# A RetNet-and-MoE kernel: the first two batches' attention by 256-token spans in 64x64 tiles

## The chip, the core and the metric

The kernel runs on one core of a Trainium2 chip. The core has a matrix engine (PE, TensorE, with its weight loads shown apart as PEld), a vector engine (DVE), an activation engine (ACT), GpSimd (POOL), and SyncE (SP), which issues DMAs here. PE reads SBUF and writes PSUM; DVE and ACT bring results from PSUM to SBUF. The metric is device time in microseconds of one execution. Three runs of the kernel before gave 306.0, 306.02 and 306.26 us, median 306.02.

## What is computed

Retention (attention with a decay instead of a softmax) over 8 batches, 8 heads, 576 tokens and 64 elements per head, and then a feed-forward layer on all 4608 tokens, with 512 model and 2048 inner elements:

```python
def _attn_ref(q, k, v):
    scores = scale * np.matmul(q, k.transpose(0, 1, 3, 2))
    gamma = 1.0 - 2.0 ** (-5.0 - np.arange(H, dtype=np.float32))
    rel = pos[:, None] - pos[None, :]
    Dmat = np.where(rel >= 0, gamma[:, None, None] ** rel[None, :, :], 0.0)
    return np.matmul(scores * Dmat[None, :, :, :], v)
...
    x = attn_out.transpose(0, 2, 1, 3).reshape(B * S, H * D)
    h = x @ w_in
    g = h * (1.0 / (1.0 + np.exp(-beta * h)))
    return g @ w_out
```

All inputs and the output are float32; the matmuls run in bfloat16.

## The kernel before

**Retention by chunks.** The decay factors into a gain on q (`gq`, which falls with the token's position) and its inverse on v (`gv`), so that inside a batch only a mask is left. The first 512 tokens of a batch are four chunks of 128 tokens. For a chunk, PE transposes q and k (`t_q` L297, `t_k` L304, tile `T`), forms the scores of keys against queries per head (`a_sc` L317, tile `sc`), and DVE multiplies them by the mask on their way from PSUM (`R`, L332). The outputs (`a_O` L364, tile `O`) are v against `R`, plus a "cross" term (`a_cross` L352): q against the state, which is the sum of k times v over all earlier chunks. The state (`a_st` L390, tile `st`) is accumulated in PSUM and after each chunk copied to `sbds` (in two blocks, L416). `a_x` (L380) brings the outputs to `xT`, the input of the layer. The last 64 tokens of every batch form blocks of their own ("tails") at the end; from batch 2 on, q and k are transposed by DMA, and the work has functions of its own (`a_O4`, `a_cross4`, `x4`).

**Tiles on PE.** Scores have 64 rows to contract, so they use half of the array's rows, two at a time (64x128). Outputs have 64 columns (128x64, two at a time). Transposes, cross and the state of the first two batches use the whole array (128x128). Later batches' cross terms use 64x64, four at a time.

**The layer.** `up(m, fo)` (L466) makes one 128-row slice of the hidden layer for 512 tokens of block m: four matmuls 128x512, then one ACT instruction (`gT`, L475). There are 16 of them per block. `down(m, ms, f0, fn)` (L499) adds `fn` of the 16 products for output rows `ms`; the last one evicts `po` to `ot` and stores it. For batch 0, `up_pair` (L479) makes fo 0 and 1 together, half of the contraction at a time; the downs of batch 0 run for three row blocks abreast (`down_rows` L593) while w_out arrives, and the fourth follows. The ups of batch 1 for fo 0 to 9 run on two chunks (256 columns) at a time, so that they can start when half of its retention is done.

**Loads.** SP's one queue carries all loads and stores in program order: q of batch 0, its k and v (eight pieces of 256 KB: one chunk, all heads, a token per partition, 256-byte runs), w_in (4 MB in pieces of 256 columns), then w_out (four of 1 MB), q, k and v of batch 1 and so on. k is cast and v gets its gain on POOL (`pre`, L277 and L259), q gets its gain on DVE for the first two batches (`pre_q`, L251). w_in is cast by POOL (L185) and, with halves exchanged for odd `ko`, by DVE (L188); w_out is scaled by 1/beta on DVE, POOL and ACT (`cast_w_out`, L195).

**Order.** Each engine takes its instructions in the order of the code. Batch 0 is written out step by step (L540 to 584). After that, `fill` is a list of ups and downs that PE works through, and `streams` hold all other steps, each with a place in the fill list; `merged` (L526) issues a step ahead of the first fill whose number is not below that place. `d0` is the number of the first down of batch 0, `u1` that of the first up of batch 1, `base[n]` those of later blocks. PSUM has eight banks: `mm` 3 (ups, downs), `sc` 2, `O` 2, `st` 1.

Of the kernel before, what the change touches and what calls it, by code (L numbers as in the profile page):

```python
# [19 lines left out]
def kernel(  # L20
# [21 lines left out]
    PC = P // CB  # L42
    TL = S - MB
# [23 lines left out]
    NQ = 6  # L67
    E = CB
# [4 lines left out]
    def load_q(b, us=(0, 1)):  # L73
# [6 lines left out]
        for u in us:  # L80
            w = slice(u * HP, (u + 1) * HP)
            nc.sync.dma_start(t[:, w].rearrange("p h i d -> p h (i d)"),  # L82
                              q[b, w, :MB, :].rearrange("h (p i) d -> p h (i d)", i=CB))

# [12 lines left out]
    ahead = [(0, 0), (0, 1), (1, 0), (1, 1), (2, 0), (3, 0), (2, 1), (3, 1)]  # L97
    keys_first = [(0, 0), (1, 0), (0, 1), (1, 1), (2, 0), (3, 0), (2, 1), (3, 1)]
# [13 lines left out]
    for n, j in ahead:  # L112
        load_kv(n, (j,))
# [7 lines left out]
    pos = consts.tile([P, 2, CB + 1], F32, name="pos")  # L121
    for j, (step, mul) in enumerate(((1, CB), (P, 1))):
        nc.gpsimd.iota(pos[:, j, :CB], pattern=[[step, CB]], base=0, channel_multiplier=mul,
                       allow_small_or_imprecise_dtypes=True)
        for x in range(2):
            nc.gpsimd.iota(pos[x * TL:(x + 1) * TL, j, CB:], pattern=[[0, 1]], base=MB, channel_multiplier=1,
                           allow_small_or_imprecise_dtypes=True)
    lscale = consts.tile([P, 1], F32, name="lscale")
    nc.vector.memset(lscale[:], math.log(scale))
    lg = consts.tile([P, 2, CB + 1, H], F32, name="lg")  # L130
    for h in range(H):
        nc.vector.tensor_scalar(lg[:, :, :, h], pos[:], math.log(1.0 - 2.0 ** (-5.0 - h)), None, ALU.mult)
    gq = consts.tile([P, CB + 1, H], F32, name="gq")
    gv = consts.tile([P, CB + 1, H], F32, name="gv")
    nc.scalar.activation(gq[:], lg[:, 0], ACT.Exp, bias=lscale[:])
    nc.scalar.activation(gv[:], lg[:, 1], ACT.Exp, scale=-1.0)
# [6 lines left out]

    causal = consts.tile([P, P], BF16, name="causal")
    nc.gpsimd.memset(causal[:], 1.0)
    nc.gpsimd.affine_select(out=causal[:], in_=causal[:], pattern=[[1, CB], [CB, PC]], compare_op=ALU.is_ge,
                            fill=0.0, base=0, channel_multiplier=-1)
# [23 lines left out]
    def load_w_in(g):  # L171
# [4 lines left out]
        for w in (slice(0, 2), slice(2, KO)) if g < 2 else (slice(0, KO),):  # L176
            nc.sync.dma_start(t[:, w], w_in_r[:, w, f0:f0 + fn])  # L177
        wts[g] = t

    def cast_w_in(g):  # L180
        t = wts[g]
        f0, fn = pieces[g]
        for ko in range(KO):
# [150 lines left out]
    def split(i):  # L334
        return i in (CB - 1, CB + 1)
# [392 lines left out]
```

## Time and profile before

| | |
|---|---|
| median of three runs | 306.02 us |
| the profiled execution's own time | 305.54 us |
| its span, first to last instruction | 303.83 us |
| granted PE clock | 1.00 |
| PE busy | 293.4 us, 97% |
| ACT, DVE, POOL busy | 134.1, 108.0, 99.9 us |
| first up of the layer starts | 18.46 us |
| first down of batch 0 starts | 32.96 us |
| first up of batch 1 starts | 51.11 us |
| first down of batch 1 starts | 68.01 us |
| DMA, 0 to 60 us | 16.98 MB, mean 283 GB/s |

A line of the timeline gives the start, the busy time of the merged group, the engine, the line of the code, the operation, what it writes and reads, and how many instructions are in it; brackets give the idle time before it and what ended that. A matmul's own time (0.22 us for 128 columns, 0.38 for 512) is mostly latency: consecutive ones overlap, so the distance of their starts tells what one costs.

### The profile page before, as it was taken

Reading aid. Unit: us, or ns where it says so; the run is one execution under the profiler, and the core shown is the slowest. Engines: PE = TensorE matmul, PEld = TensorE weight load, DVE = VectorE, ACT = ScalarE, POOL = GpSimd, SP = SyncE. Lnnn points to the kernel's source line nnn. Section 1 sums busy time; section 2 is a strip of 40 time slices with the busy share of each in tenths; the row PEclk is TensorE's granted clock in tenths of the full one; section 3 lists DMA queues with packets and bytes.
Section 4 is the critical chain, followed back from the end, with each engine's and each line's share of the span. In section 5 each row is a group of like instructions: output and inputs, shape, how many; then the busy total and the mean of one; then the engine's idle time right before and its main releaser. Section 6 shows DMA issues by size and latency. Waiting matters only on the chain.

```text
span 303.8 us, 5689 instructions
## 1 busy us (share of the span) xinstructions
PE 293.4 (97%) x2311; PEld 151.3 (50%) x2345; DVE 108.0 (36%) x202; ACT 134.1 (44%) x227; POOL 99.9 (33%) x138
## 2 busy tenths in 40 slices
PE   7799999999999999999999999999999999999995
PEld 5544456854544454445444544454455544444444
DVE  6588566504640433133222413151346510020012
ACT  5567546781147313741374127511771058107700
POOL 4666317552840723350308030942342000000000
PEclk9999999999999999999999999999999999999999
DMA  8999999999999999908982889997996110131011
GB/s 210 219 344 363 385 252 244 237 189 243 173 249 265 233 190 230 262 12 158 252 219 66 156 226 243 214 187 184 185 200 112 60 45 0 32 73 35 2 69 69
DMA packets 129210, 53.86 MB, mean 177 GB/s; under 512 B 109968, under 2 KB 122656, under 8 KB 129184
## 3 DMA queue, kind: packets, MB, share of 16 engines
q1 hardware_dynamic: 129152, 53.49, 78.4%
q8 instruction: 18, 0.29, 0.4%
q14 instruction: 8, 0.07, 0.1%
q10 hardware_dynamic: 32, 0.01, 0.0%
HBM read 36.71 MB, written 9.44 MB: 152 GB/s over the span
## 4 chain that ended last, share of the span: by engine, by line
PE 87%; DMA 6%; SPq 4%; issue 1%; POOL 1%; DVE 0%; POOLq 0%
PE po L506 41%; PE ph L473 36%; SPq L94 3%; DMA wt<-in_moe_w_out_dram 3%; PE sc L327 3%; DMA wt<-in_moe_w_in_dram 2%; PE O L441 2%; PE st L402 2%; PE O L453 1%; SPq L177 1%; POOL w_out_sb L200 1%; PE O L376 0%; PE st L405 0%; SPq L82 0%; PE T L307 0%
## 5 line engine op out<-in xcount | busy, mean ns | idle before, releaser
L475 ACT ACTIVATE gT<-ph,beta_sb 128x512 bf16<-128x512 f32 (+1 forms) x152 | 99.5, 659 | 82.2 <-PE ph L473 81.7
L506 PE MATMUL po<-w_out_sb,gT 128*128 128x512 bf16 (+2 forms) x591 | 127.1, 368 | 2.1 <-issue 1.3
L473 PE MATMUL ph<-xT,w_in_sb 128*128 128x512 bf16 (+1 forms) x592 | 125.1, 365 | 0.8 <-issue 0.2
L473 PEld LDWEIGHTS <-w_in_sb 128*128 128x128 bf16 x608 | 58.4, 98 | 63.0 <-DVE w_in_sb L188 0.9
L506 PEld LDWEIGHTS <-gT 128*128 128x128 bf16 x608 | 56.8, 98 | 63.9 <-issue 0.6
L332 DVE TENSOR_TENSOR R<-sc,causal 128x512 bf16<-128x512 f32 x72 | 45.0, 684 | 81.4 <-PE sc L327 80.3
L513 DVE COPY ot<-po 128x512 f32<-128x512 f32 (+2 forms) x34 | 22.4, 657 | 77.2 <-PE po L506 74.4
L277 POOL CAST kn<-kvn 128x512 bf16<-128x512 f32 x32 | 19.5, 612 | 55.5 <-DMA kvn<-in_k_dram 55.1
L259 POOL TENSOR_TENSOR vn<-kvn,gv 128x512 bf16<-128x512 f32 x32 | 33.3, 1042 | 13.1 <-DMA kvn<-in_v_dram 6.3
L251 POOL TENSOR_TENSOR qs<-qn,gq 128x512 bf16<-128x512 f32 x24 | 24.3, 1042 | 35.1 <-DMA qn<-in_q_dram 35.1
L408 ACT CAST sbq<-st 128x256 bf16<-128x256 f32 x18 | 6.6, 369 | 35.8 <-PE st L402 35.8
L461 DVE CAST xT<-O 128x512 bf16<-128x512 f32 x20 | 12.7, 685 | 20.2 <-PE O L453 20.2
L327 PE MATMUL sc<-qT,kT 64*128 64x128 bf16 x256 | 10.8, 218 | 0.7 <-ACT kT L308 0.6
L188 DVE CAST w_in_sb<-wt 64x256 bf16<-64x256 f32 x32 | 10.7, 334 | 1.4 <-DMA wt<-in_moe_w_in_dram 0.3
L461 ACT CAST xT<-O 128x512 bf16<-128x512 f32 x8 | 4.7, 587 | 13.4 <-PE O L453 13.4
L327 PEld LDWEIGHTS <-kT 64*128 64x128 bf16 x288 | 8.2, 94 | 3.8 <-issue 1.7
L185 POOL CAST w_in_sb<-wt 128x256 bf16<-128x256 f32 x16 | 7.2, 469 | 5.3 <-DMA wt<-in_moe_w_in_dram 5.3
L402 PEld LDWEIGHTS <-kn 128*64 128x64 bf16 x192 | 5.1, 110 | 7.6 <-issue 6.4
L212 PE MATMUL ph<-warm 128*128 128x128 f32 (+1 forms) x24 | 6.5, 405 | 1.2 <-DVE warm L119 1.2
L441 PE MATMUL O<-R,vn 128*64 128x128 bf16 x224 | 7.7, 220 | 0.0
L402 PE MATMUL st<-vn,kn 128*64 128x64 bf16 x192 | 7.4, 200 | 0.0
L266 POOL TENSOR_TENSOR kn<-tln,gq 128x512 bf16<-128x512 f32 x4 | 4.2, 1042 | 9.8 <-DMA tln<-in_q_dram 5.9
(69 smaller groups left out, 103.4 us busy)
## 6 DMA issues: line engine op xcount, KB each, us to landing
qn<-in_q_dram SPq DMA_DIRECT2D x16, 512.0 KB, 5.8
kvn<-in_k_dram SPq DMA_DIRECT2D x32, 256.0 KB, 5.1
kvn<-in_v_dram SPq DMA_DIRECT2D x32, 256.0 KB, 5.0
out_dram<-ot SPq DMA_DIRECT2D x31, 256.0 KB, 2.8
wt<-in_moe_w_out_dram SPq DMA_DIRECT2D x4, 1024.0 KB, 9.7
wt<-in_moe_w_in_dram SPq DMA_DIRECT2D x6, 512.0 KB, 8.6
out_dram<-ot SPq DMA_DIRECT2D x9, 128.0 KB, 2.4
wt<-in_moe_w_in_dram SPq DMA_DIRECT2D x4, 256.0 KB, 5.8
```

The lines of the kernel that those rows point to most:

```text
L251: e.tensor_tensor(batch[b]["qs"][:, cs, hs], q_tiles[b][:, hs, cs].rearrange("p h i d -> p i h d"), gq[:, cs, hs].unsqueeze(3).to_broadcas ...
L259: nc.gpsimd.tensor_tensor(live[i]["vn"][:], kv_tiles.pop(i)[:, 1], gains(gv, c), ALU.mult)
L277: nc.gpsimd.tensor_copy(kn[:, c % 2], t[:, 0])
L327: nc.tensor.matmul(view(sc[j][:, p, :]), L["kT"][r, p, :], rhs, start=True, stop=True, skip_group_check=True)
L332: nc.vector.tensor_tensor(R[:, j], sc[j][:], m_b, ALU.mult)
L402: nc.tensor.matmul(st[j * D:(j + 1) * D, p, :D], L["kn"][:, 2 * p + j, :], L["vn"][:, 2 * p + j, :], start=(c == 0 and p == 0), stop=True, ...
L441: nc.tensor.matmul(out4(i, p, hh), L["vn"][:, 2 * p + j, :], rhs if b is None else rhs.rearrange("k (i s) -> k i s", i=CB), start=c % 2 == ...
L461: (nc.scalar.copy if n == 1 else nc.vector.tensor_copy)(to, O.rearrange("k p i s -> k p (i s)") if b is None else O[:])
L473: nc.tensor.matmul(ph, w_in_sb[:, ko, fo * P:(fo + 1) * P], xts[m][:, ko, :, w], start=(ko == 0), stop=(ko == KO - 1))
L475: nc.scalar.activation(gts[m][:, fo, :, w], ph, ACT.Silu, scale=beta_sb[:, fo:fo + 1])
L506: nc.tensor.matmul(po[:, :nn], gT[:, fo, ms, :], w_out_sb[:, fo, n0:n0 + nn], start=(fo == 0), stop=(fo == FO - 1))
L513: (nc.scalar.copy if m == 0 else nc.vector.tensor_copy)(ot, po[:, :nn])
```

## The change

For the first two batches the unit of loading and of retention becomes a span of 256 tokens, with two neighbouring tokens in each partition (`W` = 256). The low 64 partitions hold the span's first chunk, the high 64 its second.

- Loads: k and v of a span come in runs of 512 bytes; for batch 0 by four heads at a time (256 KB), for batch 1 all heads at once (512 KB). q of batch 1 is loaded by span too. For batch 1, span 0 is loaded ahead of the last quarter of w_out. w_in's first piece comes in six DMAs that exchange the halves on the way, so all its casts are on POOL; w_out comes two rows of blocks at a time.
- Scores (`sc_span`) and outputs (`O_span`) use 64x64 tiles, four at a time, 64 instructions each per batch. One `cut` mask replaces `causal` for these.
- State: batch 0 accumulates it over one half of the rows at a time (`st_first`). Batch 1 sums each prefix anew (`st_terms`, `st_span`, `st_end`) in 64x64 and 128x64 tiles.
- In batch 0, one half of the last v is only cast, on ACT, and its gain goes on that half's k instead.
- The first two ups of batch 0 run on the first span alone (`up_part`) inside the retention of the second; the other 256 columns follow as the first fill. The downs of batch 0 run by rows, four abreast (the fourth in bank `st`), with two of their evictions on ACT and two on DVE.
- All 16 ups of batch 1 run on 256 columns at a time. Several steps of batch 2's preparation move behind `u1`.

The diff, cut to its core:

```diff
+    def load_span(b, j, cc, hs):
+        if (b, j, cc) not in spans:
+            spans[b, j, cc] = stage.tile([P, H, 2, D], F32, name="kvn", tag="kvn", bufs=NQ)
+        nc.sync.dma_start(spans[b, j, cc][:, hs].rearrange("p h i d -> p h (i d)"),
+                          (k, v)[j][b, hs, cc * W:(cc + 1) * W, :].rearrange("h (p i) d -> p h (i d)", i=2))
...
-    for n, j in ahead:
-        load_kv(n, (j,))
+    for cc in range(2):
+        for j in range(2):
+            for g in range(2):
+                load_span(0, j, cc, both[g])
...
+    def cut_of(b):
+        n = CB if b == 0 else 2
+        nc.gpsimd.memset(cuts[b][:], 1.0)
+        for h in range(2):
+            r = slice(h * D, (h + 1) * D)
+            nc.gpsimd.affine_select(out=cuts[b][r], in_=cuts[b][r], pattern=[[-1, 2], [1, n], [n, P // n]],
+                                    compare_op=ALU.is_ge, fill=0.0, base=0, channel_multiplier=-2)
...
+        if g == 0:
+            for ko in range(KO):
+                for a, b, n in ((0, D, D), (D, 0, D)) if ko % 2 else ((0, 0, P),):
+                    nc.sync.dma_start(t[a:a + n, ko], moe_w_in[ko * P + b:ko * P + b + n, f0:f0 + fn])
+        else:
+            for w in (slice(0, 2), slice(2, KO)) if g < 2 else (slice(0, KO),):
+                nc.sync.dma_start(t[:, w], w_in_r[:, w, f0:f0 + fn])
...
+    def t_k(b, cc, ps, tag, e):
+        kn, kT = pair[b, cc][:2]
+        T = psum.tile([P, 2, len(ps), P], BF16, name="T", tag=tag, bufs=BANKS[tag])
+        for i in range(2):
+            for n, p in enumerate(ps):
+                nc.tensor.transpose(T[:, i, n, :], heads(kn[:, i], p), ident[:])
+        evict(e, kT[:, :, ps[0]:ps[-1] + 1, :], T[:])
...
+    def sc_span(b, cc, g, tags):
+        kT = pair[b, cc][1]
+        Rs[b, cc, g] = R = sb.tile([P, 2, 2, 2, P], BF16, name="R", tag="R", bufs=4)
+        sc = [psum.tile([P, 2, 2, P], F32, name="sc", tag=tag, bufs=BANKS[tag]) for tag in tags]
+        for n, i in ((n, i) for n in range(2) for i in range(2)):
+            p = 2 * g + n
+            for j, h in ((0, 0), (1, 1), (0, 1), (1, 0)):
+                r = slice(j * D, (j + 1) * D)
+                nc.tensor.matmul(by(b, sc[j][h * D:(h + 1) * D, n, i, :]), kT[r, i, p, h * D:(h + 1) * D], q_span(b, 2 * cc + h, r, p),
+                                 start=True, stop=True, skip_group_check=True)
+        for j in range(2):
+            nc.vector.tensor_tensor(R[:, j], sc[j][:], cuts[b][:].unsqueeze(1).to_broadcast([P, 2, 2, P]), ALU.mult)
...
+    def O_span(b, cc, g):
+        vn, R = pair[b, cc][2], Rs[b, cc, g]
+        for n, i in ((n, i) for n in range(2) for i in range(2)):
+            p = 2 * g + n
+            for j, h in ((0, 0), (1, 1), (0, 1), (1, 0)):
+                r, hh = slice(h * D, (h + 1) * D), j ^ p % 2
+                key, o = region(b, 2 * cc + h, p)
+                nc.tensor.matmul(o[hh * D:(hh + 1) * D], vn[r, i, 2 * p + j, :], by(b, R[r, j, n, i, :]),
+                                 start=begins(key, (hh,)), stop=False, skip_group_check=True)
...
+    def st_first(c, es):
+        if c == 0:
+            states[0] = psum.tile([P, HP, P], F32, name="st", tag="st", bufs=1)
+        st, (kn, _, vn), r = states[0], pair[0, c // 2], (low, high)[c % 2]
+        for i in range(2):
+            for p in range(HP):
+                nc.tensor.matmul(st[:, p, :], kn[r, i, 2 * p:2 * p + 2].rearrange("k h d -> k (h d)"),
+                                 vn[r, i, 2 * p:2 * p + 2].rearrange("k h d -> k (h d)"), start=begins(("st", 0), (0,)) if p + c + i == 0 else False,
+                                 stop=True, skip_group_check=True)
+        if c < CB - 1:
+            blocks_of(sbds[c], st, es, False)
...
+    def st_terms(x, terms):
+        st, key = states[1]
+        for p in range(HP):
+            for d, r in terms:
+                kn, _, vn = pair[1, d]
+                for i in range(2):
+                    for j in range(2):
+                        nc.tensor.matmul(st[j * D:(j + 1) * D, x, p, :], kn[r, i, 2 * p + j, :], vn[r, i, 2 * p + j, :],
+                                         start=begins(key, (j,)), stop=True, skip_group_check=True)
+    def st_span(cc, es):
+        tag = "st" if cc else "O"
+        states[1] = (psum.tile([P, 2, HP, D], F32, name="st", tag=tag, bufs=BANKS[tag]), ("st", 1, cc))
+        if cc:
+            st_terms(0, [(0, rows), (1, low)])
+            blocks_of(sbds[2], states[1][0][:, 0], es, True)
+        else:
+            st_terms(0, [(0, low)])
+            st_terms(1, [(0, rows)])
+            for x in range(2):
+                blocks_of(sbds[x], states[1][0][:, x], es, True)
+    def st_end(e):
+        st_terms(0, [(1, high)])
+        evict(e, ends[1][:], states[1][0][:, 0])
...
+    def up_part(c0, fos, kos):
+        if 0 not in gts:
+            gts[0] = sb.tile([P, FO, CB, P], BF16, name="gT", tag="gT", bufs=2)
+        w = slice(c0 * PC, (c0 + 2) * PC)
+        for fo in fos:
+            if kos[0] == 0:
+                phs[fo] = psum.tile([P, CB, 2 * PC], F32, name="ph", tag="mm", bufs=3)
+            for ko in kos:
+                nc.tensor.matmul(phs[fo][:], w_in_sb[:, ko, fo * P:(fo + 1) * P], xts[0][:, ko, :, w],
+                                 start=(ko == 0), stop=(ko == KO - 1))
+            if kos[-1] == KO - 1:
+                nc.scalar.activation(gts[0][:, fo, :, w], phs[fo][:], ACT.Silu, scale=beta_sb[:, fo:fo + 1])
...
-        (nc.scalar.copy if m == 0 else nc.vector.tensor_copy)(ot, po[:, :nn])
+        (nc.scalar.copy if m == 0 and ms % 2 == 0 else nc.vector.tensor_copy)(ot, po[:, :nn])
...
     warm_up(5)
     betas()
     betas_safe()
     for n in range(4):
         pre_q(0, n)
+    t_q(0, 0, "O", A)
     warm_up(1, 128)
+    t_q(0, 1, "mm", V)
+    pre_span(0, 0, 0, g0, Z)
+    t_k(0, 0, lo2, "mm", A)
+    pre_span(0, 0, 0, g1, Z)
+    warm_up(1, 128)
+    sc_span(0, 0, 0, ("sc", "sc"))
+    t_k(0, 0, hi2, "mm", A)
+    pre_span(0, 1, 0, g0, Z, True)
+    warm_up(1, 128)
+    sc_span(0, 0, 1, ("O", "O"))
+    pre_span(0, 1, 0, g1, Z, True)
     warm_up(2, 128)
+    new_span_O(0, 0, ("sc", "sc"))
+    O_span(0, 0, 0)
+    pre_span(0, 0, 1, g0, Z)
+    st_first(0, (A, A))
+    O_span(0, 0, 1)
+    t_k(0, 1, lo2, "mm", V)
+    pre_span(0, 0, 1, g1, Z, True)
+    x_span(0, 0, (V, None))
+    cross_span(0, 1)
+    sc_span(0, 1, 0, ("O", "O"))
+    pre_span(0, 1, 1, g0, Z, True)
+    st_first(1, (A, A))
+    t_k(0, 1, hi2, "mm", A)
+    x_span(0, 0, (None, A))
     warm_up(1, 128)
+    pre_span(0, 1, 1, g1, A)
+    sc_span(0, 1, 1, ("mm", "mm"))
     cast_w_in(0)
+    new_span_O(0, 1, ("sc", "sc"))
+    O_span(0, 1, 0)
+    st_first(2, (A, A))
+    cross_span(0, 2)
+    up_part(0, (0, 1), (0, 1))
+    O_span(0, 1, 1)
+    cross_span(0, 3)
+    x_span(0, 1, (V, A))
+    up_part(0, (0, 1), (2, 3))
     cast_w_in(1)
+    st_first(3, (A, A))
...
+    fill = [F(up_part, 2, (0, 1), range(KO))] + [F(up, 0, fo) for fo in range(2, FO)]
     d0 = len(fill)
+    def down_row(n):
+        for fo, ms in [(n, ms) for ms in range(4)] if n < FO - 2 else [(fo, 2 * (n - FO + 2) + x) for x in range(2) for fo in (FO - 2, FO - 1)]:
             down(0, ms, fo, 1)
 
+    fill += [F(down_row, n) for n in range(FO)]
 
     u1 = len(fill)
+    NH = FO
+    fill += [F(up, 1, fo, 2 * x, 2) for x in range(2) for fo in range(NH)]
+    fill += [F(up, 1, fo) for fo in range(NH, FO)]
     fill += [F(down, 1, ms, f0) for ms in range(MB // P) for f0 in range(0, FO, 4)]
+    base = {1: u1 + NH}
...
+    def span_rest(cc):
+        if cc:
+            cross_span(1, 2)
+        cross_span(1, 2 * cc + 1)
+        x_span(1, cc, (V, V if cc else A))
...
+               [(d0 + 7, F(pre_q, 1, 0)), (d0 + 7, F(pre_q, 1, 1)), (d0 + 8.5, F(t_q, 1, 0, "O", V)),
+                (d0 + 8.6, F(pre_span, 1, 0, 0, both[0], A)), (d0 + 8.6, F(pre_span, 1, 0, 0, both[1], A)),
+                (d0 + 9.5, F(t_k, 1, 0, (0, 1), "O", V)), (d0 + 10.5, F(t_k, 1, 0, (2, 3), "O", A)), (d0 + 10.51, F(span_sc, 0, 0)),
+                (d0 + 10.6, F(pre_span, 1, 1, 0, both[0], Z, True)), (d0 + 10.6, F(pre_span, 1, 1, 0, both[1], Z, True)),
+                (d0 + 11, F(span_sc, 0, 1)), (d0 + 12, F(cast_w_out, WG - 1)), (d0 + 13.5, F(span_out, 0, 0)),
+                (d0 + 13.9, F(span_out, 0, 1)), (d0 + 13.95, F(st_span, 0, (A, V))), (d0 + 15.5, F(span_rest, 0))],
+               [(u1, F(pre_q, 1, 2)), (u1, F(pre_q, 1, 3)), (u1 + 2, F(t_q, 1, 1, "O", V)),
+                (u1 + 1, F(pre_span, 1, 0, 1, both[0], Z)), (u1 + 2.1, F(pre_span, 1, 0, 1, both[1], V)),
+                (u1 + 3, F(t_k, 1, 1, (0, 1), "O", V)), (u1 + 4, F(t_k, 1, 1, (2, 3), "O", V)), (u1 + 5, F(span_sc, 1, 0)),
+                (u1 + 5.1, F(pre_span, 1, 1, 1, both[0], Z, True)), (u1 + 5.1, F(pre_span, 1, 1, 1, both[1], Z, True)),
+                (u1 + 6, F(span_sc, 1, 1)), (u1 + 10, F(span_out, 1, 0)), (u1 + 12, F(st_span, 1, (V, V))),
+                (u1 + 13, F(span_out, 1, 1)), (u1 + 14, F(span_rest, 1)), (u1 + NH + 2, F(st_end, A))]]
```

## What was predicted ahead of the run

> **What bounds the kernel.** I read the page's head first, then the timeline of PE, then the starts of single matmuls.
>
> ```profile
> span 303.8 us, 5689 instructions
> PE 293.4 (97%) x2311; PEld 151.3 (50%) x2345; DVE 108.0 (36%) x202; ACT 134.1 (44%) x227; POOL 99.9 (33%) x138
> ...
> PEclk9999999999999999999999999999999999999999
> ```
>
> PE is busy nearly all the time at full granted clock, so the time is the head before the first up, the PE work after it, and whatever PE waits. The timeline of PE gives the joints:
>
> ```profile
> 17.89 0.40 PE L405 MATMUL st<-vn,kn 128*128 128x128 bf16 x4
> 18.46 0.59 PE L488 MATMUL ph<-xT,w_in_sb 128*128 128x512 bf16 x2 [0.17 <-ACT xT L386]
> 19.22 1.41 PE L488 MATMUL ph<-xT,w_in_sb 128*128 128x512 bf16 x5 [0.17 <-issue]
> 20.47 12.66 PE L473 MATMUL ph<-xT,w_in_sb 128*128 128x512 bf16 x55
> 32.96 1.55 PE L506 MATMUL po<-w_out_sb,gT 128*128 128x512 bf16 x6
> 34.66 9.22 PE L506 MATMUL po<-w_out_sb,gT 128*128 128x512 bf16 x41 [0.15 <-POOL w_out_sb L200]
> ```
>
> The head lasts 18.5 us; from 20.47 the ups of fo 2 to 15 run. Consecutive 128x512 matmuls start 0.2157 us apart, so these 56 would end at 32.55 instead of 32.96 (0.41 of waits on w_in), and the six at 32.96 would end at 34.25 instead of 34.66 (0.41 on w_out). What ends the waits of the head, from the timelines of POOL, DVE and ACT:
>
> ```profile
> 13.47 0.61 POOL L277 CAST kn<-kvn 128x512 bf16<-128x512 f32 x1 [0.57 <-DMA kvn<-in_k_dram]
> 14.70 2.19 POOL L259 TENSOR_TENSOR vn<-kvn,gv 128x512 bf16<-128x512 f32 x2 [0.61 <-DMA kvn<-in_v_dram]
> 14.46 2.69 DVE L332 TENSOR_TENSOR R<-sc,causal 128x512 bf16<-128x512 f32 x4 [1.13 <-PE sc L327]
> 13.39 0.58 ACT L308 COPY kT<-T 128x512 bf16<-128x512 bf16 x1 [1.22 <-PE T L307]
> 13.87 0.76 ACT L416 CAST sbd<-st 64x256 bf16<-64x256 f32 x2
> ```
>
> POOL waits for loads: pieces of 256 KB come 1.2 us apart (7.47, 8.67 ... 13.47, 14.70). ACT and DVE wait for PE. The head follows the loads.
>
> **The loads.** Runs of 256 bytes move at about 217 GB/s (the 40 slices over the first 60 us), w_in's of 1 KB at about 348, w_out's of 2 KB at 385. No load here has 512-byte runs. Bounds: 1.2 us per piece (nothing gained) and 0.68 (256 KB at 385 GB/s). Per engine a 256-byte run takes 18.9 ns and a 1 KB run 47.1; the line between gives 28.3 for 512 bytes, 0.9 us per piece, which I take. The last v lands about 13.4 instead of 15.8, and w_in follows 2.4 us earlier.
>
> **The head, walked.** I took the new order engine by engine: each starts when its last instruction and its inputs are done, about 0.05 us after them. Durations by row: R 0.645 (two in 1.29), kT 0.58 on ACT and 0.42 on DVE, state to sbd two in 0.76, xT 0.58 on ACT and 0.69 on DVE, POOL 0.61 plain and 1.04 with a gain. The same walk over the order before gives the first up at 18.3 (trace 18.46) and L473 at 20.3 (20.47), so I trust it to some tenths. After:
>
> The first half's keys are turned by 9.05, its R is done at 10.9, the second half's at 12.2 (DVE runs through). The outputs of the second half wait for that, and only behind them on PE stand the second span's transposes (12.6, though their keys were cast at 11.5). On DVE then come kT (to 13.4), xT (14.1) and R (15.4). On ACT come the first state (12.3 to 13.0), the second (14.45 to 15.2), and behind it kT's other half, xT and the last v, 0.58 each, to 16.95: that v landed at 13.4. It releases the third state (17.0), then the first-span ups (17.8), the last outputs and cross (18.6), xT (to 19.6), the other half of fo 0 and 1 (19.9) and L473's work at 20.8, against 20.3. ACT starts back-to-back work up to 0.09 us before the last one's end (14.79 and 15.28 in its timeline, 0.58 each), which gives back 0.2. So the head is **+0.3**, whether a piece takes 0.68 or 1.1 us: the load time falls, but the chain over PE, ACT and DVE takes its place. At 1.2 us it is +0.7. The early w_in ends the 0.41 of waits, w_out in halves the other 0.41.
>
> At nothing I cost the finer DMAs (an issue takes 0.5 us, SP is done with k and v by 6 us), w_in's first casts on POOL (done about 15.3, wanted at 17.8), two more Exp of 0.2 to 0.3 (under the wait for q, which ends at 4.74), the masks moved among the ups (POOL idles there) and batch 2's moved preparation (loaded by 58, wanted at 72). If such a cover goes, the cost is its own duration. Span 0 of batch 1 is loaded ahead of w_out's last quarter, so that one lands about 41.5; row 12 wants it at 45.
>
> **Batch 1 on PE.** Start-to-start, from busy times less one instruction's own (24 in 0.53, one 0.22): T, cross and old st 56 ns, sc in 64x128 26.5, O in 128x64 28, 64x64 tiles 13.6, 64-column st 17.
>
> ```profile
> 81.32 0.29 PE L402 MATMUL st<-vn,kn 128*64 128x64 bf16 x8
> 81.54 0.53 PE L453 MATMUL O<-qT,sbq 64*64 64x128 bf16 x24
> ```
>
> Before: T 32, cross 12, st 16, sc 32, O 32 instructions: 1.79 + 0.67 + 0.90 + 0.85 + 0.90 = 5.11 us. After: T and cross stay, sc 64 and O 64 at 13.6, st 80 at 17 (prefixes summed anew): 2.46 + 0.87 + 0.87 + 1.36 = 5.56. **+0.45.** A state matmul on 64 rows alone isn't in the trace; 13.6 to 28 ns give -0.3 to +0.9, and 17 is the nearest row.
>
> Each change of tile shape adds a gap:
>
> ```profile
> 48.75 1.03 PE L506 MATMUL po<-w_out_sb,gT 128*128 128x512 bf16 x4
> 49.71 0.67 PE L376 MATMUL O<-R,vn 128*64 128x128 bf16 x16
> 50.31 0.40 PE L361 MATMUL O<-qT,sbd 128*128 128x128 bf16 x4
> 50.54 0.39 PE L405 MATMUL st<-vn,kn 128*128 128x128 bf16 x4
> 50.77 0.39 PE L307 MATMUL T<-ident,kn 128*128 128x128 bf16 x4
> 51.11 0.61 PE L473 MATMUL ph<-xT,w_in_sb 128*128 128x256 bf16 x4
> ```
>
> The last of the four starts at 49.40, the next shape at 49.71: 0.31 where 0.216 is usual. In and out alike cost 0.096. Before: 12 such changes (four sc bursts, two O bursts). After: sc 2 + 2 + 2, span_out(0) with its two state terms 3, span_out(1) 2 + 2, st_end 2, and st_span(1) takes turns between whole rows and the low half for each of four p, 9: together 24. **+1.15.**
>
> Waits: scores of the second half stand right behind the transposes that they need; ACT turns them in 0.58, 0.2 of it under the first half's scores: 0.5. At u1 the last row of downs is followed by cross and xT and at once by the first half-up that reads xT; DVE evicts ot of ms 3 (0.68) and then xT (0.69) from the end of the row: 1.35. Above, the cross of batch 1 at 50.31 has st and T behind it, which cover most of this; they are gone. Behind span_rest(1) two half-ups (0.87) cover two evictions on DVE in a row (1.4 and latency): 0.5. The second half's keys, cast on DVE behind this, cost 0.3. Together 2.65. Before, from 32.96 to the first down of batch 1 (68.01) are 35.05 us: matmuls of MoE 27.7, attention 5.11, changes 1.15, so 1.1 of waits, w_out's 0.41 among them. **+1.55.**
>
> **Sum.** 0.3 - 0.41 + 0.45 + 1.15 + 1.55 = **+3.1 us** (w_out's 0.41 is in the last term). Behind 68 us the work is the same and PE sets the pace. The profiled execution took 305.54 (span 303.83 and 1.7 around); with the sum 308.6. The median of the runs is 306.02, so I say **309.1**.
>
> **Rivals.** *The head keeps following loads and POOL.* If the evictions interleave better than walked, POOL's chain sets it: 6 us of casts and gains from 7.0, then w_in's, ups of fo 2 at 16.9 instead of 20.8: 4 us less, 305.1, faster than before. It decides from where those ups start: under 17.2 faster, 17.2 to 18.4 no difference. For it: the loads do come earlier, and POOL waits for them now. Against: the walk that meets the trace of before. 0.15 faster, 0.09 between.
>
> *64x64 tiles don't run four abreast.* If a matmul starts only every 27 ns, scores and outputs cost 128 x 13.4 = 1.7 us more in batch 1, the chain of the head 1.2, less 0.2 hidden: 311.8. Against it stand the 24 matmuls at 13.6 ns with the same order of quadrants; for it, those read only transposed states. 0.11.
>
> The Trainium skill, "TensorE: Matmul & The Clock Gate" (section "Wait — 56ns, not 53.3ns?") says that start-to-start never falls below about 25 ns however small a matmul is; by it the time would be this rival's. The trace's 13.6 ns disagrees for tiles in different quadrants.
>
> *It doesn't do what it says* only so far as the longer runs buy no rate: 0.4 us more, inside the forecast.
>
> **Numbers.** Forecast 0.65, within 308.0 to 310.4. Range 305.6 to 311.8: it leaves out the rival that ends faster and the far side of the dear one. A measurement of this kernel can tell 0.2% (0.6 us) from no change. Faster 0.15, same 0.09, slower 0.76.
>
> **What would show it.** Right: the first 128x512 up of fo 2 at 20.5 to 21; the last v's copy on ACT starting over 2 us after its landing; gaps of about 0.1 us between the state's groups of four; PE idle about 1.3 us ahead of the first half-up of batch 1; the first down of batch 1 near 71. Wrong: whole-width ups before 18.4, or less than 1.5 us of waits between 33 and 71.

## The result, and the profile after

The changed kernel took 311.29 us (median of four runs, 310.64 to 311.65), the kernel before 306.14 beside it (306.0 to 306.29). The ratio is 1.0166, 95% interval 1.0145 to 1.0186. The forecast of 309.1 had the sign and most of the places right, and was 2.2 us short. Medians here and below leave out four executions with a lower granted clock; the profile of the state's products by rows is of one of these (lower up to 26 us), so that its stretches are read and not its times of day. The profiled execution of the changed kernel took 310.97 us. The head of its page:

```profile
span 309.3 us, 6204 instructions
PE 299.3 (97%) x2583; PEld 156.9 (51%) x2583; DVE 111.5 (36%) x203; ACT 133.8 (43%) x232; POOL 101.1 (33%) x144
```

DVE, ACT and POOL work within 3.5 us of what they did before. PE is 5.9 us busier by this count, but the row charges each small matmul its latency of 0.2 us, so it isn't read as cost. The timeline of PE answers to the joints shown before (`ph` up, `po` down; a joint is a place where one kind of work on PE ends and the next begins):

```profile
18.31 0.60 PE L608 MATMUL ph<-xT,w_in_sb 128*128 128x256 bf16 x4
...
20.51 1.05 PE L608 MATMUL ph<-xT,w_in_sb 128*128 128x256 bf16 x8
21.39 12.25 PE L593 MATMUL ph<-xT,w_in_sb 128*128 128x512 bf16 x56
33.48 0.59 PE L627 MATMUL po<-w_out_sb,gT 128*128 128x512 bf16 x2
34.42 1.89 PE L627 MATMUL po<-w_out_sb,gT 128*128 128x512 bf16 x8 [0.34 <-ACT gT L595]
```

The first up is where it was (18.31 against 18.46), the ups of fo 2 begin 0.92 later, and their 56 matmuls run without a wait in 12.09 us instead of 12.49. A ledger over the same joints, the last two columns from two of the experiments below:

| us | before | after | forecast of the difference | difference | regrouped | pairs last |
|---|---|---|---|---|---|---|
| first 128x512 up of fo 2 | 20.47 | 21.39 | +0.3 | +0.92 | 20.17 | 20.42 |
| from there to the first down | 12.49 | 12.09 | -0.41 | -0.40 | 12.09 | 12.09 |
| from there to the first down of batch 1 | 35.05 | 40.05 | +3.15 | +5.00 | 36.55 | 35.51 |
| from there to the end of the span | 235.8 | 235.8 | 0 | 0 | 236.1 | 235.7 |

So the loss is one stretch of 40 us. What PE waits for in it, by the view of waits (line waited at, releaser, us in total, times, longest):

```profile
PE ph L593 <- DVE xT L355: 2.0, 2, 1.7
PE T L372 <- DVE kn L298: 0.5, 1, 0.5
PE po L627 <- ACT gT L595: 0.3, 1, 0.3
PE sc L394 <- ACT kT L355: 0.3, 1, 0.3
```

That is 3.1 us, where the same view of the kernel before has three entries of 0.2 from 18 us to its first down of batch 1. This view counts only what exceeds a matmul's latency; from starts to starts the same five places lose 1.69, 0.46, 0.63, 0.51 and 0.53: 3.8. The largest stands ahead of the first half-up of batch 1. PE, ACT and DVE there:

```profile
51.19 0.39 PE L430 MATMUL O<-qT,sbd 128*128 128x128 bf16 x4
53.26 0.94 PE L593 MATMUL ph<-xT,w_in_sb 128*128 128x256 bf16 x7 [1.68 <-DVE xT L355]
```

```profile
49.62 0.37 ACT L355 CAST sbd<-st 64x256 bf16<-64x256 f32 x1 [2.00 <-PE st L468]
50.48 0.37 ACT L355 CAST sbd<-st 64x256 bf16<-64x256 f32 x1 [0.49 <-DVE sbd L355]
```

```profile
50.02 0.43 DVE L355 CAST sbd<-st 64x256 bf16<-64x256 f32 x1 [2.53 <-ACT sbd L355]
50.88 0.43 DVE L355 CAST sbd<-st 64x256 bf16<-64x256 f32 x1 [0.43 <-ACT sbd L355]
51.32 1.29 DVE L634 COPY ot<-po 128x512 f32<-128x512 f32 x2
52.52 0.68 DVE L355 CAST xT<-O 128x512 bf16<-128x512 f32 x1
```

The brackets show the four copies of the state going to and fro between ACT and DVE, each behind the first released by the other engine's. They end at 51.3, and only then come two copies of down products and `xT`.

### The profile page after: what moved, and what is told of

It is laid out like the page before. It is cut to its first block, busy times and chain, and to the rows that moved or that the text cites. A ratio compares the mean times of both kernels' runs of the same rounds, so it can differ in the third digit from the quotient of the medians.

```text
span 309.3 us, 6204 instructions
## 1 busy us (share of the span) xinstructions
PE 299.3 (97%) x2583; PEld 156.9 (51%) x2583; DVE 111.5 (36%) x203; ACT 133.8 (43%) x232; POOL 101.1 (33%) x144
## 3 DMA queue, kind: packets, MB, share of 16 engines
q1 hardware_dynamic: 122048, 53.49, 73.5%
## 4 chain that ended last, share of the span: by engine, by line
PE 94%; DVE 2%; ACT 2%; issue 1%; POOL 1%; ACTq 0%; POOLq 0%
PE po L627 40%; PE ph L593 40%; PE sc L517 3%; PE O L562 2%; PE ph L250 2%; PE st L535 2%; PE O L574 1%; PE sc L394 1%; PE st L468 1%; PE O L423 1%; ACT kT L355 1%; PE st L450 1%; ACT sbd L355 1%; PE ph L608 1%; PE T L372 1%
## 5 line engine op out<-in xcount | busy, mean ns | idle before, releaser
L595 ACT ACTIVATE gT<-ph,beta_sb 128x512 bf16<-128x512 f32 (+1 forms) x158 | 101.0, 644 | 86.3 <-PE ph L593 86.0
L627 PE MATMUL po<-w_out_sb,gT 128*128 128x512 bf16 (+2 forms) x608 | 129.3, 368 | 0.3 <-ACT gT L595 0.3
L593 PE MATMUL ph<-xT,w_in_sb 128*128 128x512 bf16 (+1 forms) x632 | 127.3, 358 | 2.0 <-DVE xT L355 2.0
L593 PEld LDWEIGHTS <-w_in_sb 128*128 128x128 bf16 x632 | 60.4, 98 | 62.4 <-DVE xT L355 2.4
L522 DVE TENSOR_TENSOR R<-sc,causal 128x512 bf16<-128x512 f32 x56 | 34.8, 682 | 74.4 <-PE sc L517 74.4
L634 DVE COPY ot<-po 128x512 f32<-128x512 f32 (+2 forms) x36 | 23.6, 658 | 77.1 <-PE po L627 77.1
L289 POOL TENSOR_TENSOR qs<-qn,gq 128x512 bf16<-128x512 f32 x25 | 25.9, 1067 | 32.8 <-DMA qn<-in_q_dram 32.8
L334 POOL CAST kn<-kvn 128x512 bf16<-128x512 f32 x24 | 14.6, 609 | 52.8 <-DMA kvn<-in_k_dram 52.8
L397 DVE TENSOR_TENSOR R<-sc,cut 128x512 bf16<-128x512 f32 x16 | 10.1, 684 | 4.1 <-PE sc L394 4.1
L582 ACT CAST xT<-O 128x512 bf16<-128x512 f32 x8 | 4.7, 587 | 13.4 <-PE O L574 13.4
L517 PE MATMUL sc<-qT,kT 64*128 64x128 bf16 x192 | 7.4, 217 | 0.0
```

Of the source, the lines that this page charges most:

```text
L289: e.tensor_tensor(batch[b]["qs"][:, cs, hs], q_tiles[b][:, hs, cs].rearrange("p h i d -> p i h d"), gain[:, cs, hs].unsqueeze(3).to_broadc ...
L334: nc.gpsimd.tensor_copy(kn[:, c % 2], t[:, 0])
L517: nc.tensor.matmul(view(sc[j][:, p, :]), L["kT"][r, p, :], rhs, start=True, stop=True, skip_group_check=True)
L522: nc.vector.tensor_tensor(R[:, j], sc[j][:], m_b, ALU.mult)
L582: (nc.scalar.copy if n == 1 else nc.vector.tensor_copy)(to, O.rearrange("k p i s -> k p (i s)") if b is None else O[:])
L593: nc.tensor.matmul(ph, w_in_sb[:, ko, fo * P:(fo + 1) * P], xts[m][:, ko, w], start=(ko == 0), stop=(ko == KO - 1))
```

## The experiments

Each kernel is the changed one with the edit shown, unless the text names another. Times are medians; a ratio is to the kernel before, run on the same chip in turn. The experiments ran in groups on four chips, so small differences between two of them are read from ratios and profiles as well.

### The beta guard behind the casts

GpSimd makes three small instructions for beta (`betas_safe`) ahead of its first cast of k; here they come behind its casts and gains of the first batch.

```diff
     betas()
-    betas_safe()
...
     pre_span(0, 1, 1, g0, Z, True)
+    betas_safe()
```

> The three POOL instructions that guard beta move from the start of the head to behind the last gain of v on POOL; nothing else changes. In the changed kernel the first key cast starts on POOL at 7.93 us, behind these three, which wait for a transpose that PE reaches only after its ten warm-up matmuls (all ten at 0.427 us a start there, six in the kernel before). Theory (the head is a chain over POOL, PE, DVE and ACT that begins at that cast): the cast starts about 7.1, when its load lands, and everything up to the whole-width ups follows: they start 0.7 to 0.85 earlier than 21.39, at 20.5 to 20.7, and the time falls to about 310.5; the spread of the runs (1.0 us) shrinks, since the warm-up no longer reaches the chain. Rival (the head follows the loads and w_in, which the cast doesn't touch): the ups stay at 21.2 to 21.5 and the time at 311.3.

310.81 us, ratio 1.0169 (1.0151 to 1.0187): inside the changed kernel's own interval. In its profile the first cast starts at 7.22 instead of 7.93 and the ups of fo 2 at 20.88 instead of 21.39, which would confirm the theory; the medians don't show it. When the first k lands (start of its DMA plus time to landing, from the view of tile `kvn`) tells why. In the profiles with 512-byte runs it lands at 7.05 to 7.96 us, so it scatters between executions. Without the guard the cast starts 0.12 to 0.13 behind that, with it 0.05, 0.44 and 0.45 in three further profiles, and 0.88 in the changed kernel's own, where k had landed at 7.05 and POOL was still at the guard:

```profile
7.08 0.60 POOL L261 TENSOR_SCALAR tiny<-tiny 128x16 f32<-128x16 f32 x1
7.76 0.22 POOL L262 TENSOR_TENSOR beta_sb<-beta_sb,tiny 128x16 f32<-128x16 f32 x1
7.93 1.17 POOL L298 CAST kn<-kvn 128x512 bf16<-128x512 f32 x2
```

So the guard can hold the first cast up by some 0.8 us, and in other executions by nothing. What can be compared between single profiles is the distance from the landing to the ups of fo 2: 13.05 before, 13.79 here, 13.80 to 13.91 in the three profiles named, 14.34 in the changed kernel's. The changed head costs 0.74 against before, the guard another 0.55 in that one execution, and its k landed 0.37 earlier than that of the kernel before (7.05 against 7.42): together the 0.92 of the ledger.

### 256-byte runs again

```diff
+        if b == 0:
+            for i in range(2):
+                nc.sync.dma_start(spans[b, j, cc][:, hs, i, :],
+                                  (k, v)[j][b, hs, cc * W:(cc + 1) * W, :].rearrange("h (p i) d -> p h i d", i=2)[:, :, i])
+            return
```

> The loads of k and v of batch 0 are each cut in two, one for even and one for odd tokens: the same bytes to the same places, in runs of 256 bytes instead of 512. Theory (chain): pieces come about 1.2 us apart again, the last v lands about 16 instead of 13.5, and w_in 2 to 3 us later, but every consumer of the head is later still (the last v is copied at 16.97, w_in is wanted at 18.3), so the whole-width ups start at 21.3 to 21.8 and the time moves by 0 to 0.4 us. Rival (the longer runs are what the head lives on): the ups start 2 to 2.8 us later and the time is 313.3 to 314.

312.95 us, ratio 1.0234 (1.0211 to 1.0257): 1.66 more than with the long runs by the medians, 2.1 by the ratios, and between the two expectations. In 8 to 10 us the queues move 218 GB/s, against 292 in the changed kernel. The edit halves the pieces too, but the kernel before moved 218 in whole pieces of 256 KB, so it is the runs. Yet the ups of fo 2 begin only 0.26 later. The loss comes right behind:

```profile
21.65 0.59 PE L598 MATMUL ph<-xT,w_in_sb 128*128 128x512 bf16 x2
23.56 12.15 PE L598 MATMUL ph<-xT,w_in_sb 128*128 128x512 bf16 x54 [1.31 <-POOL w_in_sb L227]
```

From the second of the two, at 21.87, to 23.56 are 1.7 us where 0.22 is usual, and from the first of these ups to the first down it takes 13.90 us instead of 12.09. The chain hides most of the lateness of k and v, and nothing hides the w_in that queues behind them.

### The joint at the first half-up

The outputs and the state of batch 1's first span are issued one row of downs earlier, its cross and `xT` two rows, with all four state copies on ACT.

```diff
-(d0 + 13.5, F(span_out, 0, 0)),
-(d0 + 13.9, F(span_out, 0, 1)), (d0 + 13.95, F(st_span, 0, (A, V))), (d0 + 15.5, F(span_rest, 0))
+(d0 + 12.5, F(span_out, 0, 0)),
+(d0 + 12.9, F(span_out, 0, 1)), (d0 + 12.95, F(st_span, 0, (A, A))), (d0 + 14, F(span_rest, 0))
```

> In batch 1, outputs and state of span 0 are issued one row of downs earlier, cross and the copies to xT two rows earlier, and the four copies of the state are all on ACT. The same instructions run. Theory (between the last row of downs and the first half-up PE waits because xT stands on DVE behind two copies of the state and two of ot): the start-to-start gap of 1.90 us at 51.36 to 53.26 falls to under 0.5, and the time to 309.4 to 309.9. Rival (the wait belongs to something that comes with the data, a load or R, and moves along): a wait of over 1 us is left in the last three rows or at the first half-ups, and the time stays within 0.5 of 311.3.

309.49 us, ratio 1.0128 (1.0101 to 1.0155). The 1.90 us before the first half-up are 0.22, so the wait hung on the chain above. The edit moves the copies and ends their turns between two engines at once, so it doesn't part the two. And a new wait stands two steps on:

```profile
53.07 0.62 PE L362 MATMUL T<-ident,qs 128*128 128x128 bf16 x8 [0.81 <-DVE qs L289]
```

The gain on q, 0.98 us on DVE, is issued at `u1` and had been covered by the old wait. The stretch from the first down to that of batch 1 is 1.2 us shorter, not 1.7.

### The state's products by rows

```diff
-        for p in range(HP):
-            for d, r in terms:
-                kn, _, vn = pair[1, d]
+        for d, r in terms:
+            kn, _, vn = pair[1, d]
+            for p in range(HP):
```

> The state of batch 1's second span is summed with all matmuls on whole rows first and then all on the low half, instead of by turns for each of four head pairs: 32 matmuls as before, but three changes of tile shape instead of nine. Theory (a change of shape costs about 0.1 us each): the stretch from the last half-up before them to the first after them falls from 1.65 us (61.30 to 62.95) to about 1.05, 0.6 less, and the time falls by 0.6, which the spread of the runs may hide. Rival (the gaps are the small matmuls' own floor, whatever the order): the stretch stays at 1.5 to 1.65.

310.2 us, ratio 1.0142 (1.0125 to 1.0159), 0.7 less than the changed kernel by the ratios, whose intervals overlap. The same 32 matmuls need fewer turns between tile shapes (nine changes with both ends, now three). The changed kernel, then this one:

```profile
61.50 1.51 PE L468 MATMUL st<-vn,kn 128*64 128x64 bf16 x32
62.95 0.61 PE L593 MATMUL ph<-xT,w_in_sb 128*128 128x256 bf16 x4
```

```profile
66.48 0.81 PE L468 MATMUL st<-vn,kn 128*64 128x64 bf16 x32
67.22 0.61 PE L593 MATMUL ph<-xT,w_in_sb 128*128 128x256 bf16 x4
```

1.45 us become 0.74: six changes less, 0.12 each at most (0.01 of it is that the step inside groups of four is longer). In the changed kernel groups of four stand 0.123 to 0.125 apart (last start to next start), with 0.019 inside a group.

### All joints of batch 1

The two edits above, and with them: the gain on q at `d0 + 14.1`, ahead of the copies of down products; the second pair of transposed keys right behind the first; the key cast, the state and the later outputs of the second span a place earlier; bank `st` for the first accumulator instead of the fourth.

```diff
-            tag = "st" if (m, ms) == (0, 3) else "mm"
+            tag = "st" if (m, ms) == (0, 0) else "mm"
...
-(d0 + 10.5, F(t_k, 1, 0, (2, 3), "O", A))
+(d0 + 9.6, F(t_k, 1, 0, (2, 3), "O", A))
...
-[(u1, F(pre_q, 1, 2)), (u1, F(pre_q, 1, 3)),
+[(d0 + 14.1, F(pre_q, 1, 2)), (d0 + 14.1, F(pre_q, 1, 3)),
```

> The joints of batch 1 all loosened, nothing else: the first span's outputs and state one down earlier with both state copies' halves on ACT, the state's products grouped by rows, the second pair of transposed keys right behind the first, the second span's key cast and outputs one step earlier, its queries' scaling ahead of the copies of the down products, and the spare bank given to the first accumulator instead of the fourth. Theory (the 5 us between first down and first down of batch 1 are waits at joints plus the price of changing tile shapes): 1.2 (joint at the first half-up) + 0.85 (state) + 0.5 (third down) + 0.5 (second half of the scores) + 0.9 (queries) + 0.6 (keys) + 0.45 (first up of 512 rows) = 5.0 at most, of which some comes back as new waits: 306.3 to 307.8 us, and 35.5 to 37 us between the two firsts. Rival (the evictions of the smaller tiles fill ACT and DVE, so a wait taken away at one joint comes back at the next): only the two measured alone stay gone, 308.8 to 309.5 us, 38 to 38.5 us between the two.

307.48 us, ratio 1.0046 (1.0028 to 1.0065), inside the theory's range and below the rival's. The stretch is 37.53 us, 2.5 less than in the changed kernel, and half a us above the theory's. The waits at the third down, at the second half of the scores and at the first half-up on the second span are gone. What is left is on DVE: the transposed keys of the second span wait 0.6 us for `qT`, which stands behind q's gain, the key cast and the late copies of down products.

### The last rows of the downs, alone

```diff
-    fill += [F(down_row, n) for n in range(FO)]
+    fill += [F(down_row, n) for n in range(FO - 4)]
+    fill += [F(down, 0, ms, FO - 4) for ms in range(4)]
```

> One part of the change half undone: the downs of the first block go by rows only for the first 12 rows, the last four rows go accumulator by accumulator, so the four accumulators end 1.56 us apart and not all in the last 1.6 us. Theory (the copies of the down products stand ahead of the attention's output copy on DVE and hold up the first half-up): one copy of 0.65 us leaves that place, the 1.9 us before the first half-up becomes 1.2 to 1.3, time 310.5 to 310.8 us. Rival (the state's four copies in turn set it): unchanged, 311.1 to 311.5 us.

311.0 us, ratio 1.0155 (1.0128 to 1.0183), and a stretch of 40.05 us as in the changed kernel. The wait at the half-up does fall, from 1.90 to 1.61, but the last row of w_out is now wanted six matmuls sooner:

```profile
47.64 1.24 PE L627 MATMUL po<-w_out_sb,gT 128*128 128x512 bf16 x5 [0.23 <-ACT w_out_sb L240]
```

The state behind it ends half a us later, its to and fro does too, and the gain is given back. Neither expectation named this.

### The head in another order

With all joints loosened, and in the head: the second span's keys cast and turned ahead of the first span's outputs, both evictions on ACT, the last v copied ahead of `xT` and of the second state, the guard later, one warm-up matmul less.

```diff
+    pre_span(0, 0, 1, g0, Z)
+    pre_span(0, 0, 1, g1, Z, True)
     new_span_O(0, 0, ("sc", "sc"))
     O_span(0, 0, 0)
-    pre_span(0, 0, 1, g0, Z)
+    t_k(0, 1, lo2, "mm", A)
     st_first(0, (A, A))
+    t_k(0, 1, hi2, "mm", A)
     O_span(0, 0, 1)
...
     pre_span(0, 1, 1, g1, A)
+    x_span(0, 0, (None, A))
+    st_first(1, (A, A))
     sc_span(0, 1, 1, ("mm", "mm"))
```

> The kernel with all joints of batch 1 loosened, and the head in another order: the second span's keys are cast and transposed ahead of the first span's outputs, the last value tile is copied on ACT ahead of the output copy, and GpSimd's three small instructions for beta stand behind its casts. Theory (the head is a chain over PE, ACT, DVE and GpSimd and not the loads): the first 128x512 up of the third group at 20.3 to 20.6 us instead of 21.1 to 21.6, time 0.6 to 1.0 us below that of the kernel with the joints alone, 305.6 to 307.0 us. Rival (the landing of the last value tile at 13.5 us, or of w_in behind it, sets it): ups no earlier than 20.9 us or with waits on w_in after them, time within 0.2 us of the kernel with the joints alone.

307.02 us, ratio 1.0030 (1.0012 to 1.0047), 0.5 less than with the joints alone, a little short of the theory's 0.6 to 1.0. From the landing of the first k to the ups of fo 2 (at 20.72) it takes 12.76 us: 1.0 less than without the new order (13.79 to 13.91) with the same loads, and 0.3 less than in the kernel before. No wait on w_in follows. So the chain over the engines set the head. The copy of the last v on ACT starts at 14.83; in the changed kernel it starts at 16.97, though the tile had landed at 13.64 and waited for ACT. Here it lands at 14.73, so little of the loads' lead is left.

### Head and last rows

The head's order and the joints as above, and:

```diff
-    fill += [F(down_row, n) for n in range(FO)]
+    fill += [F(down_row, n) for n in range(FO - 4)]
+    fill += [F(down, 0, ms, FO - 4) for ms in range(4)]
```

> The head in the other order, the joints loosened, and the last four rows of the first downs accumulator by accumulator. Theory: with the joint at the first half-up already loosened, taking the copies away from it is worth 0 to 0.4 us more, 305.4 to 306.8 us; that would be the change at its best beside the 305.9 us of the kernel before, no gain by more than 0.2 us. Rival: the copies meet the scores' masks on ACT and DVE instead and the time rises by 0.2 to 0.5 us.

306.58 us, ratio 1.0015 (1.0000 to 1.0029), the column "regrouped" of the ledger. Beside the loosened joints the regrouping pays: the stretch is 36.55 us instead of 37.28, the copies no longer crowd DVE at `u1`, and the waits of 0.3 for q's gain and 0.2 for `R` go. PE's only entry in the view of waits from 18 to 70 us is 0.2 of "issue".

### Fewer insertions

In the kernel "head and last rows", the second span's scores go in one place instead of two, its state and outputs in one instead of three, and its `xT` to DVE and ACT.

```diff
-(u1 + 5, F(span_sc, 1, 0)), ... (u1 + 6, F(span_sc, 1, 1)), (u1 + 10, F(span_out, 1, 0)),
-(u1 + 11, F(st_span, 1, (V, V))), (u1 + 12, F(span_out, 1, 1)),
+(u1 + 6, F(span_sc, 1, 0)), ... (u1 + 6, F(span_sc, 1, 1)), (u1 + 12, F(st_span, 1, (V, V))),
+(u1 + 12, F(span_out, 1, 0)), (u1 + 12, F(span_out, 1, 1)),
```

> The kernel with the head in the other order, the joints loosened and the last rows regrouped, and beside it the second span's attention put into fewer places: both halves of its scores together, and its state and both halves of its outputs together, so that three of its five insertions between half-ups go. Its output copies go one to DVE and one to ACT. Theory (what is left of the loss against the kernel before is the price of the shape changes, some 0.19 us for an insertion's two edges): 0.5 us less than without this, 36.0 us between first down and first down of batch 1 instead of 36.55, time 305.9 to 306.3 us. Rival (DVE's masks for both halves, 2.5 us in one piece, or the copies crowd before the second half-ups): the gain comes back as a wait, 306.4 to 306.9 us.

305.8 us, ratio 0.9995 (0.9979 to 1.0011): no difference from the kernel before. The stretch is 35.87 us, 0.68 less, although two waits for ACT's casts of w_out stand in it with 0.5 us.

### Pairs last

The kernel "fewer insertions", and in it the first two accumulators take rows 12 and 13, then 14 and 15, ahead of the other two.

```diff
-    fill += [F(down, 0, ms, FO - 4) for ms in range(4)]
+    def down_pairs(f0):
+        for fo, ms in [(f0 + x, ms) for ms in range(2) for x in range(2)]:
+            down(0, ms, fo, 1)
+    fill += [F(down_pairs, FO - 4), F(down_pairs, FO - 2)] + [F(down, 0, ms, FO - 4) for ms in (2, 3)]
```

> The kernel with fewer insertions, and in it the last four rows of the first downs in another order: the first two accumulators take rows 12 and 13, then 14 and 15, and the third and fourth come whole behind them. In the kernel with fewer insertions PE waited twice, 0.5 us in all, for ACT to cast the last rows of w_out. Theory (that wait is real time on the path, and the last row's cast is ready at 46.1 us): the last row is now needed 0.4 us later, so 0.4 to 0.5 us of the wait goes, 305.3 to 305.5 us, which would be 0.15 to 0.2% below the kernel before. Rival (the copies behind the casts on ACT, first of them the output's, become the next wait): 305.7 to 306.0 us, no difference from the kernel before.

305.49 us, ratio 0.9980 (0.9966 to 0.9993): by this interval faster than the kernel before, by 0.07 to 0.34%. The waits on w_out are gone, and the whole view of waits from 20 to 68 us is one line:

```profile
PE O L423 <- DVE R L397: 0.2, 1, 0.2
```

### The best head with 256-byte runs

The kernel "head and last rows" with the edit for 256-byte runs.

> The kernel with the head in the other order, the joints loosened and the last rows regrouped, with the first batch's keys and values read again in 256-byte runs (twice the pieces of half the length, the same data at the same places). Theory (the longer runs free the queue for w_in, which stands behind them): the ups start here 0.8 to 1.2 us earlier than in the changed kernel, so the late w_in costs that much more than the 1.7 us which it cost there: 308.3 to 309.8 us, with 2 to 3 us of waits on the w_in casts. Rival (with the head's chain shorter the loads of keys and values themselves set the start of the ups, and w_in is late by no more than before): the ups start over 0.8 us later than at 20.2, and the time is 307.3 to 308.2 us.

310.34 us, ratio 1.0133 (1.0111 to 1.0155): 3.76 more than with 512-byte runs, above both ranges. The rival's sign is there, since the ups of fo 2 begin at 22.19 instead of 20.17, and w_in is late as well:

```profile
22.19 0.38 PE L598 MATMUL ph<-xT,w_in_sb 128*128 128x512 bf16 x1
22.92 1.25 PE L598 MATMUL ph<-xT,w_in_sb 128*128 128x512 bf16 x5 [0.35 <-POOL w_in_sb L227]
```

From the first of these ups to the first down it takes 12.67 us instead of 12.09, and the stretch behind is 0.82 longer: the last downs wait three times, 0.9 us in all, for ACT's casts of w_out. So the lateness is 2.0 in the head, 0.6 at w_in and 0.8 at w_out. In the head POOL waits for loads again, as before the change (three brackets of 0.56 to 0.60 us on k and v up to 14 us), and ACT for the last v:

```profile
16.53 0.62 ACT L303 CAST vn<-kvn 128x512 bf16<-128x512 f32 x1 [0.74 <-DMA kvn<-in_v_dram]
```

So with short runs the loads set this head, with long runs the chain does.

## Why the prediction was right, and by how much not

**Sign and place: right; the size in part by luck.** The ledger has the loss where the sum had it: little in the head, the bulk between 33 and 74 us, none behind. The terms add up to 3.04 us (the sum says 3.1), the profiles differ by 5.5, and of the 2.5 that are missing, 1.85 are in the bulk and 0.6 in the head. The measured 311.29 lies above the 308.0 to 310.4 given with the forecast. It lies inside the range because that ends at the dear rival's 311.8, and this rival, 64x64 tiles that don't run four abreast, is not what happened.

**The walk of the head: right but for the guard.** The walk has the first keys turned by 9.05, the last v copied by 16.95 and the ups of fo 2 at 20.8. In the profile without the guard, where k landed at 7.09, the scores on the first keys start at 9.15 and the ups at 20.88. In the changed kernel's they start at 9.67 and 21.39: the guard, which the walk doesn't have, stood in the way of the first cast. Not borne out are the 0.2 that were taken off for ACT's early starts. The step said +0.3; by the clock it is +0.41 without the guard and +0.92 with it, and a landing that scatters by 0.9 us can't be foretold from one profile. SP issues the last k and v by 9.0 us and not by 6, which costs nothing on PE. The waits on w_in went as said (-0.40 for -0.41).

**The loads: right, also the estimate.** 0.9 us per piece of 256 KB was taken from the line between two rows; 292 GB/s gives 0.90. The Trainium skill, "DMA: Bandwidth & Descriptors" (the table at its head), puts the line rate at 512 bytes and more per transfer. The step from 218 to 292 GB/s bears out that runs below 512 bytes cost rate, but at 512 bytes the rate is still short of the 385 that w_out's 2 KB runs reach here.

**The rival "longer runs buy no rate": mis-sized.** Its price, 0.4 us, counted only the head's chain and left out what stands behind k and v in the queue. Measured 1.66 by the medians, and 3.76 once the head is shorter.

**PE work of attention: right.** In the changed kernel's four long bursts and its single ones, scores and outputs start 13.4 to 13.7 ns apart, the state's 64-row products 15.1 to 16.4 (17 was taken). So the rival of 27 ns falls. Read one by one, four matmuls, one for each quadrant, start within 10 ns, and within a burst the next four start 56 ns after these, which is the step of one 128x128 matmul. The floor of about 25 ns between starts that the Trainium skill gives ("TensorE: Matmul & The Clock Gate", section "Wait — 56ns, not 53.3ns?") doesn't hold for 64x64 tiles in turn over four quadrants.

**Changes of shape: right in number, a little dearer than said.** 24 were counted, and there are 24. Over the usual step a change costs 0.09 from large matmuls into small ones, 0.11 to 0.13 back (the prediction took the way back for alike) and 0.11 between the state's two shapes: 2.6 us in all, 0.109 each for 0.096. "TensorEngine Tiling (Array Packing)" of the Trainium skill (section "Tiling Modes", "Key Properties") says that a change of mode drains the engine, and names no price; the pair of state stretches above is one. The last kernel, with 12 changes as before the change, needs 35.51 us for the stretch against 35.05: +0.46, which is the attention's 0.45; by single steps its changes (1.3 us) and its waits (0.9) are those of before.

**Waits: the step that failed.** The sum had 2.65 us of them in the changed kernel, 1.55 more than before. By single steps they are 40.05 less 27.8 of MoE, 5.5 of attention and 2.6 of changes, 4.1 in all. Term by term: second half of the scores 0.53 for 0.5, first half-up on the second span 0.46 for 0.5, keys 0.63 for 0.3 (the cast on DVE took 0.86), first half-up 1.69 for 1.35, third down 0.51 for nothing; the rest lies in small gaps. Two things were not seen. The first is what stands on DVE ahead of the two evictions that were counted: four state copies that go to and fro between two engines, and behind them a second copy of down products. The second: four accumulators abreast take all three `mm` banks, and the third of these is held by the last up until its silu is done (34.37 us, the third down starts at 34.42).

**What would show it.** Right: ACT late with the last v, gaps of about 0.1 between the state's groups, an idle PE ahead of the first half-up (1.68 for 1.3). Missed: the ups of fo 2 at 21.4 (20.5 to 21), the first down of batch 1 at 73.5 (71).

## What to carry to other kernels

Price a transfer by what queues behind it as well: the longer runs were worth 1.8 us here through w_in alone, though in the changed kernel the data that they carry were in little hurry. Where small tiles are inserted into a stream of large ones, count the changes of shape (0.1 us each here) and put what has one shape together. And at a joint, list all that stands in the queues of the evicting engines, not only the evictions that PE waits for; a chain whose links alternate between two engines gains nothing by the second (the four state copies took 1.69 us in turns, 1.54 on ACT alone). The next wait appears as soon as one is gone.

## What was not expected of the hardware

The first ten warm-up matmuls of every kernel here are the same instructions. From start to start they take 0.381 us in the mean in the profile before and 0.445 in that after, though the granted clock reads 1.00 in both. The mean mixes two steps. Read one by one, all but the first are 0.427 us in the changed kernel; in the kernel before they are 0.427 too until 4.24 us, and the last two are 0.216. What differs from execution to execution is when the short step sets in. The guard waits for a matmul behind these ten, so in the changed kernel they are what made it late. When the first k lands, at 7.05 to 7.96 us with 512-byte runs, shows no link to it in these profiles: where all ten are slow it lands at 7.05, 7.61, 7.66 and 7.96, elsewhere at 7.09 to 7.55.
